# Gated mix of two attentions on one core: the first ten projection tiles take turns among four PSUM banks, the gate goes by the Pool engine and a transfer, and the main part's banks get pools of their own

## The chip, the cores and the metric

The kernel runs on one core of a Trainium2 chip. The time is the device time of that core in microseconds; lower is better. The engines are the tensor engine (PE, with its weight loads PEld), the vector engine (DVE), the scalar engine (ACT), GpSimd (POOL) and the sync engine (SP), which issues nearly all DMA transfers. Each engine takes its own instructions in the order in which the program wrote them, and waits on semaphores for what others make.

## What is computed

One input x of 2048 positions by 448 features goes through two attention blocks of 16 heads of 28, and a gate mixes the two. Everything is float32.

```python
g = sigmoid((x * gate_w).sum(-1))              # one number per position
# A: local and dilated: each position sees 8 keys, 2 apart, backwards
a = softmax(q·k[pos - 2w], w = 0..7) v  @ wo_A
# B: full attention over all 2048 keys
b = softmax(q k^T / sqrt(28)) v  @ wo_B
out = g * a + (1 - g) * b
```

The matmuls run in a reduced format of float32, so a product is made from a high and a low part of each operand: high times high, high times low, low times high.

## The kernel before

The order of every engine's work is written out by hand (`manual_schedule`); the program text is the order. There are three stages.

**Stage 1, projections.** 92 tiles are made one after another. Tiles 0 to 27 are queries and keys of B (128 rows by 512 positions each), 28 to 43 the values of B, 44 to 91 queries, keys and values of A (128 positions by 448 columns). The first ten (`FULL = 10`) are projected whole by `project`: eleven products of 128 rows, in the order of the lists `FIRST` (tile 0) or `ORDER`. Product (a, c, k) multiplies part a of x (0 high, 1 low) with part c of the weights, piece k of the 448 features; piece 3 is the tail of 64 features, whose high and low parts lie in the two halves of one tile. From tile 10 on, `project_halves` makes two chains of products of 64 rows that run beside each other, and mixes in matmuls of a first pass over the scores (`s1_half`, line 141), whose row maxima DVE takes (line 158). That first pass needs the keys, which have gone to DRAM and come back as `KH` (`load_k`).

A tile's result lies in a PSUM tile of two banks. There are four of them, `PS[0]` to `PS[3]`, named r0 to r3 in the profile's instructions (the page leaves the number out). Projections use r0 and r1 in turn (`PJ`), the first pass r2 and r3 (`PM`). A result of the first ten tiles leaves by `qk_tile`: ACT copies the high part (line 332), DVE makes the low part (line 333), SP stores both. Later results leave by one ACT copy (lines 337 and 351) and POOL adds the two halves (lines 339 and 352).

Before a tile can run, its operands must be split: `split` copies the high part on ACT (line 206) and subtracts on DVE or POOL (line 207). `split_x(nb)` does this for a quarter of x, its tail last (lines 232, 234); `split_third` for the third group of columns of the first weights. In program order `split_third` stands ahead of tile 1, `split_x(1)` ahead of tile 0's products. 13 matmuls on zeros (line 197) run while the first operands are still on their way.

**The gate.** The sums of the sigmoid come out of tiles 44 to 59 into `zt`. After tile 64, ACT makes exp(-z) and exp(z) (line 493), DVE adds 1 and inverts, twice (lines 494, 495); this gives `g_t` and `omg` = 1 - g, 128 by 16. After tile 68, PE transposes `omg` into the bank pair of the next tile, ACT copies it out (line 500), SP stores it to DRAM (`og_scr`, line 501) and loads it back in another layout, `og`, by 16 transfers (line 504). `load_q(0)` for the main part follows after tile 69.

**Stage 2, the main part.** 16 units of 16 steps make B's attention: score matmuls (line 1000), the exponential on ACT (line 1003), the sums over the values (`do_av`, line 962), with the rest of the first pass beside them, and A's attention on POOL and DVE. Its PSUM tiles T (three pairs of banks and a single one) come from one pool that takes the place of r0 to r3; `av` has the eighth bank. `RP[0]` is the pair that lies on r2, `RP[1]` that on r0, `TP` that on r1; T1 and av lie on r3.

**Stage 3** makes the output projection.

## Time and profile before

| what | value |
|---|---|
| time, median of 3 runs | 930.05 us (928.61 to 930.82) |
| the profiled execution's own time | 928.69 us |
| its span, first to last instruction | 926.9 us |
| busy share PE, DVE, ACT, POOL | 99%, 79%, 70%, 67% |
| mean granted clock of PE | 0.997 |
| stage 1 | 0 to 259 us |

In the views below, a row gives the start in us, the time it took in us, the engine, the line, the operation, what it writes and reads with shapes, how many instructions were merged (x4), and in square brackets the idle time of the engine before it and what ended that. "r" is a PSUM tile of stage 1, "T" one of the main part. In a row of windows stand the window, its length, and the busy time with the number of instructions for PE, then the granted share of PE's clock, the share of the DMA engines and GB/s.

### The profile page before, as it was taken

What the parts mean: (1) busy time and instruction counts of PE and PEld (TensorE: products, weight loads), DVE (VectorE), ACT (ScalarE), POOL (GpSimd) and SP (SyncE); (2) the same over time, 40 slices, a digit from 0 to 9 for tenths busy, and PEclk for the clock granted to TensorE, in tenths of its full rate; (3) what the DMA queues carried; (4) which work ended last, traced back from release to release, by engine and by line L of the source; (5) the groups of instructions that cost most, each with busy time, mean ns of one, the idle gap of its engine ahead of it and who ended that gap; (6) DMA issues with size and microseconds to landing.
All of it is one profiled execution on the core that took longest, in us unless ns stands there. A gap on an engine that the chain in (4) does not pass through costs nothing.

```text
span 926.9 us, 21402 instructions
## 1 busy us (share of the span) xinstructions
PE 914.1 (99%) x8398; PEld 545.6 (59%) x8398; DVE 733.3 (79%) x979; ACT 651.7 (70%) x802; POOL 620.8 (67%) x483
## 2 busy tenths in 40 slices
PE   8999999999999999999999999999999999999998
PEld 6899999989944444444444444444444444466667
DVE  5588999989969999999999999999998888500012
ACT  5456434333368888888888888888989889855551
POOL 2389846454469699999999999999994851300100
PEclk9999999999999999999999999999999999999999
DMA  9877402545362341336135232421312123553422
GB/s 285 263 232 196 156 12 81 152 100 147 85 239 62 95 125 45 85 104 134 41 92 152 88 101 60 133 82 30 106 42 53 33 62 99 149 159 110 135 88 91
DMA packets 101222, 104.36 MB, mean 113 GB/s; under 512 B 61732, under 2 KB 71348, under 8 KB 100336
## 3 DMA queue, kind: packets, MB, share of 16 engines
q1 hardware_dynamic: 100976, 102.72, 38.5%
q8 instruction: 66, 1.08, 0.5%
q10 hardware_dynamic: 144, 0.26, 0.1%
q14 instruction: 36, 0.29, 0.1%
HBM read 61.99 MB, written 40.48 MB: 111 GB/s over the span
## 4 chain that ended last, share of the span: by engine, by line
PE 92%; DMA 3%; ACT 2%; SPq 2%; DVE 1%; issue 1%; POOL 0%; ACTq 0%; DVEq 0%; POOLq 0%
PE T L1000 30%; PE av L962 26%; PE r L290 15%; PE T L801 8%; PE r L285 5%; PE r L141 4%; PE T L141 4%; DMA qk_hi<-qkh 1%; ACT P L1003 1%; SPq L98 1%; PE T L779 1%; DMA V<-in_xT 1%; DMA onlo<-on_lo 1%; DMA KH<-qk_hi 0%; DVE MX L145 0%
## 5 line engine op out<-in xcount | busy, mean ns | idle before, releaser
L1003 ACT ACTIVATE P<-T 128x1024 f32<-128x1024 f32 x512 | 497.1, 1024 | 91.9 <-PE T L1000 90.3
L145 DVE TENSOR_REDUCE MX<-T 128x1 f32<-128x512 f32 x470 | 443.4, 954 | 42.0 <-PE T L141 16.8
L962 PE MATMUL av<-P,V 128*32 128x512 f32 x2048 | 273.6, 606 | 0.0
L1000 PEld LDWEIGHTS T<-QH,KH 30*128 30x128 f32 x1024 | 91.0, 182 | 231.2 <-ACT P L1003 199.8
L1000 PE MATMUL T<-QH,KH 30*128 30x512 f32 x1024 | 220.9, 492 | 2.9 <-ACT P L1003 1.6
L141 PE MATMUL T<-KH,QP 28*128 28x512 f32 x704 | 222.0, 461 | 0.0
L158 DVE TENSOR_REDUCE MX<-r 128x2 f32<-128x1024 f32 x160 | 191.6, 1222 | 25.4 <-PE r L141 20.9
L1000 PE MATMUL T<-QH,KL 28*128 28x512 f32 x1024 | 188.7, 394 | 0.0
L1000 PE MATMUL T<-QL,KH 28*128 28x512 f32 x1024 | 187.3, 393 | 0.0
L597 POOL TENSOR_TENSOR prod<-qt,kt 128x896 f32<-128x896 f32 x64 | 135.2, 2116 | 5.6 <-DMA kt<-a_scr 5.2
L351 ACT ACTIVATE raw<-r 128x896 f32<-128x896 f32 (+1 forms) x64 | 58.9, 921 | 99.0 <-PE r L290 99.0
L652 POOL TENSOR_TENSOR oat<-oat,prod 128x896 f32<-128x896 f32 x56 | 118.1, 2109 | 2.4
L141 PEld LDWEIGHTS T<-KH,QP 28*128 28x128 f32 x704 | 86.2, 182 | 23.4 <-ACT P L1003 14.0
L352 POOL TENSOR_TENSOR ast<-raw 128x448 f32<-128x448 f32 x48 | 55.5, 1157 | 60.5 <-ACT raw L351 47.7
L647 POOL TENSOR_TENSOR prod<-vt,L 128x896 f32<-128x896 f32 x56 | 95.4, 1704 | 0.6
L141 PE MATMUL r<-KH,QP 64*128 64x512 f32 x320 | 94.2, 391 | 1.2 <-DVE MX L158 0.7
L1000 PEld LDWEIGHTS T<-QL,KH 28*128 28x128 f32 x1024 | 92.8, 185 | 0.0
L1000 PEld LDWEIGHTS T<-QH,KL 28*128 28x128 f32 x1024 | 92.0, 183 | 1.0
L290 PE MATMUL r<-wh,xh 64*128 64x448 f32 (+1 forms) x512 | 86.7, 363 | 1.0 <-ACT omT L500 1.0
L962 PEld LDWEIGHTS av<-P,V 128*32 128x32 f32 x2048 | 40.3, 108 | 78.8 <-issue 73.9
L789 DVE TENSOR_TENSOR oalo<-T,oah 128x384 fp32r<-128x384 f32 x16 | 8.9, 558 | 90.9 <-ACT onhi L788 82.3
L290 PE MATMUL r<-wh,xl 64*128 64x448 f32 (+1 forms) x384 | 70.8, 363 | 0.0
(111 smaller groups left out, 1148.3 us busy)
## 6 DMA issues: line engine op xcount, KB each, us to landing
a_scr<-ast SPq DMA_DIRECT2D x24, 448.0 KB
qk_hi<-qkh SPq DMA_DIRECT2D x24, 256.0 KB
qk_lo<-qkh SPq DMA_DIRECT2D x24, 256.0 KB
rbc<-rs SPq DMA_DIRECT2D x60, 64.0 KB
QP<-qk_hi SPq DMA_DIRECT2D x64, 56.0 KB
KL<-qk_lo SPq DMA_DIRECT2D x16, 224.0 KB
QH<-qk_hi SPq DMA_DIRECT2D x64, 56.0 KB
QL<-qk_lo SPq DMA_DIRECT2D x64, 56.0 KB
```

The source lines that it names most:

```text
L141: nc.tensor.matmul(bank, qhis[u][h % 2][r, 128 * qs:128 * qs + 128], KH[u // NB % 3][r, 512 * kc:512 * kc + 512], start=True, stop=True)
L145: nc.vector.tensor_reduce(MX[:, n % NMX:n % NMX + k], bank, axis=X, op=ALU.max)
L158: nc.vector.tensor_reduce(m, PM[k], axis=X, op=ALU.max)
L290: nc.tensor.matmul(bank[:, 0:cols], x, ws[c][rows, k, 0:cols], start=first, stop=last)
L351: nc.scalar.activation(raw[:, :, 0:cols], PJ[n % 2][:, :, 0:cols], AF.Copy)
L597: nc.gpsimd.tensor_tensor(out=p, in0=qt[c], in1=kvt["k", c % 2][:, HALO - DIL * w:HALO - DIL * w + NJ, :], op=ALU.mult)
L647: nc.gpsimd.tensor_tensor(out=dst.rearrange("p j (h d) -> p j h d", d=DH), in0=kvt["v", c % 2][:, HALO - DIL * w:HALO - DIL * w + NJ, :].r ...
L652: nc.gpsimd.tensor_tensor(out=oat[c], in0=oat[c], in1=oat[c, w], op=ALU.add)
L801: writes(bank, nc.tensor.matmul(bank[:, :D], src, wo[c][:, k, :], start=(first and k == ks[0] and i == 0), stop=(last and k == ks[-1] and ...
L962: nc.tensor.matmul(av[32 * h:32 * h + 32, :], V[:, kt, 4 * g + h, :], tiles_[h], start=(kt == 0), stop=(kt == NJ - 1), skip_group_check=True)
L1000: nc.tensor.matmul(bank[a], (KH[g % 3], KH[g % 3], KL[g % 2])[t][r, ks], (qh, ql, qh)[t][r, :], start=(t == 0), stop=(t == 2))
L1003: nc.scalar.activation(p, RP[0] if a == "2" else mine, AF.Exp, scale=SCALE)
```

## The change

1. **Four banks.** The first ten tiles use `PS[n % 4]` in place of `PJ[n % 2]`.
2. **Order at the start.** The 13 matmuls on zeros become 9, then the first product of tile 0, then 3. `FIRST` alternates high and low weights and puts the tail's products last. The third piece of the first x is cast by ACT, not DVE; DVE makes the three low parts first and the tail's after them. `split_third` stands ahead of tile 0's products, `split_x(1)` behind tile 0's result.
3. **First pass, first tile.** In tile 11 (`S1_START`) the score matmuls stand four (the first of each chain) and one (the second) products later.
4. **Gate.** POOL adds the 1 (it reads it from V, which holds ones there); one inversion stands after tile 66, one after tile 68; the transpose and ACT's copy go; `omg` is stored as it lies, element by element, after tile 70; the 16 loads of `og` stand after tile 73, `load_q(0)` after tile 76.
5. **Pools.** T[0], T[1], T[2] have a pool each; T1 and av share one.

```diff
-    def banks(shapes, ctx_):
-        pool = ctx_.enter_context(tc.tile_pool(name=f"t{len(T)}", bufs=1, space=bass.MemoryType.PSUM))
-        T[:] = [pool.tile([128, *x, 512], F32, name=f"T{len(x)}_{i}") for i, x in enumerate(shapes)]
+    def banks(n):
+        for i in range(n):
+            pool = ctx.enter_context(tc.tile_pool(name=f"t{i}", bufs=1, space=bass.MemoryType.PSUM))
+            T.append(pool.tile([128, 2, 512], F32, name=f"T{i}"))
...
-    for _ in range(13):
-        nc.tensor.matmul(PM[1][:, 1, :], t0[:, 128:256].bitcast(F32R), t0.bitcast(F32R), start=True, stop=True)
+    def warm(n):
+        for _ in range(n):
+            nc.tensor.matmul(PM[1][:, 1, :], t0[:, 128:256].bitcast(F32R), t0.bitcast(F32R), start=True, stop=True)
+
+    warm(9)
...
-        FIRST = [(a, c, k) for a, c in ((0, 0), (0, 1)) for k in range(3)] + [
-            (1, 0, 0), (0, 0, 3), (0, 1, 3), (1, 0, 1), (1, 0, 2)]
+        FIRST = [(0, 0, 0), (0, 1, 0), (0, 0, 1), (0, 1, 1), (0, 0, 2), (0, 1, 2),
+                 (1, 0, 0), (1, 0, 1), (1, 0, 2), (0, 0, 3), (0, 1, 3)]
...
-            bank = PJ[n % 2][:, half or 0, :]
+            bank = PS[n % 4][:, 0, :] if half is None else PJ[n % 2][:, half, :]
...
                 product(n, p, None, i == 0, i == len(order) - 1)
+                if n == 0 and i == 0:
+                    warm(3)
...
                         if s1[m - n]:
-                            l[8:8] = [(m, s1_half, (1, half))]
-                            l[2:2] = [(m, s1_half, (0, half))]
+                            late = m == S1_START
+                            l[8 + late:8 + late] = [(m, s1_half, (1, half))]
+                            l[2 + 4 * late:2 + 4 * late] = [(m, s1_half, (0, half))]
...
-                bank = PJ[n % 2][:, 0, :]
+                bank = PS[n % 4][:, 0, :]
...
-        for kt in range(3):
+        for kt in range(2):
             nc.vector.tensor_copy(xh[0][:, kt, :], r[:, kt, :])
+        nc.scalar.activation(xh[0][:, 2, :], r[:, 2, :], AF.Copy)
...
-            if n == 1:
+            if n == 0:
                 split_third()
-            if n in (0, 3, 5):
-                split_x((n + 1) // 2 if n else 1)
+            if n in (3, 5):
+                split_x((n + 1) // 2)
...
                 a_tile(n, t[2], t[3])
+            if n == 0:
+                split_x(1)
...
             if n == 64:
+                gate = []
                 for sgn, dst in ((-1.0, g_t), (1.0, omg)):
                     e = sp.tile([128, NJ], F32, name="ez")
                     nc.scalar.activation(e, zt, AF.Exp, scale=sgn)
-                    nc.vector.tensor_scalar(e, e, 1.0, None, op0=ALU.add)
-                    nc.vector.reciprocal(dst, e)
-            if n == 68:
-                b = PJ[(n + 1) % 2][:, 0, :]
-                nc.tensor.transpose(b[0:NJ, 0:128], omg, ident)
-                t = wp.tile([NJ, 128], F32, name="omT", bufs=1)
-                nc.scalar.activation(t, b[0:NJ, 0:128], AF.Copy)
-                nc.sync.dma_start(og_scr.rearrange("(j p) -> j p", j=NJ), t)
+                    nc.gpsimd.tensor_tensor(out=e, in0=e, in1=V[:, 0, :, DH], op=ALU.add)
+                    gate.append((dst, e))
+            if n in (66, 68):
+                nc.vector.reciprocal(*gate.pop(0))
+            if n == 70:
+                nc.sync.dma_start(og_scr.rearrange("(j p) -> p j", j=NJ), omg)
+            if n == 73:
                 for b in range(NB):
...
-            if n == 69:
+            if n == 76:
                 load_q(0)
...
-    banks([(2,), (2,), (2,), ()], ctx)
+    banks(3)
     RP = T[2], T[0]
-    TP, T1 = T[1], T[3]
-    av = ctx.enter_context(tc.tile_pool(name="psv", bufs=1, space=bass.MemoryType.PSUM)).tile(
-        [128, 512], F32, name="av")
+    TP = T[1]
+    pool = ctx.enter_context(tc.tile_pool(name="psv", bufs=1, space=bass.MemoryType.PSUM))
+    T1 = pool.tile([128, 512], F32, name="T1")
+    av = pool.tile([128, 512], F32, name="av")
```

PE at the start, before: the zeros (r3 from t0), then tile 0 into r0, tile 1 into r1, tile 2 into r0 again. xh0 and xl0 are the high and low part of the first quarter of x, wh0 and wl0 those of the weights.

```order
L197 MATMUL r3_140<-t0_161 128x512 x13
L285 MATMUL r0_128<-xh0_184,wh0_192 128x512 x3
L285 MATMUL r0_128<-xh0_184,wl0_193 128x512 x3
L285 MATMUL r0_128<-xl0_188,wh0_192 128x512
L285 MATMUL r0_128<-xh0_184,wh0_192 128x512
L285 MATMUL r0_128<-xh0_184,wl0_193 128x512
L285 MATMUL r0_128<-xl0_188,wh0_192 128x512 x2
L285 MATMUL r1_132<-xh0_184,wh0_192 128x512 x4
L285 MATMUL r1_132<-xh0_184,wl0_193 128x512 x4
L285 MATMUL r1_132<-xl0_188,wh0_192 128x512 x3
L285 MATMUL r0_128<-xh0_184,wh0_192 128x512 x4
```

The same place now:

```order
L200 MATMUL r3_140<-t0_161 128x512 x9
L290 MATMUL r0_128<-xh0_180,wh0_188 128x512
L200 MATMUL r3_140<-t0_161 128x512 x3
L290 MATMUL r0_128<-xh0_180,wl0_189 128x512
...
L290 MATMUL r0_128<-xl0_184,wh0_188 128x512 x3
L290 MATMUL r0_128<-xh0_180,wh0_188 128x512
L290 MATMUL r0_128<-xh0_180,wl0_189 128x512
L290 MATMUL r1_132<-xh0_180,wh0_188 128x512 x4
...
L290 MATMUL r2_136<-xh0_180,wh0_188 128x512 x4
...
L290 MATMUL r3_140<-xh1_181,wh0_188 128x512 x4
```

Tile 0's tail products now end its list, and tile 2 begins in r2, which no result holds, where before it began in r0.

ACT at the same place, before: the weights' first group (raw), the second quarter of x (xh1), tile 0's result (qkh from r0), then the third weights.

```order
L206 ACTIVATE wh0_192<-raw_196 128x128 x3
L206 ACTIVATE xh1_185<-V_146 128x512 x3
L232 ACTIVATE xh1_185<-V_146 128x512
L332 ACTIVATE qkh_257<-r0_128 128x512
L206 ACTIVATE wh0_192<-raw_196 128x128 x3
L206 ACTIVATE wh0_192<-wt0_195 128x128
L332 ACTIVATE qkh_281<-r1_132 128x512
```

And now:

```order
L211 ACTIVATE wh0_188<-raw_192 128x128 x6
L211 ACTIVATE wh0_188<-wt0_191 128x128
L340 ACTIVATE qkh_256<-r0_128 128x512
L211 ACTIVATE xh1_181<-V_146 128x512 x3
L237 ACTIVATE xh1_181<-V_146 128x512
L340 ACTIVATE qkh_280<-r1_132 128x512
```

The third weights moved ahead of tile 0's result, the second quarter of x behind it.

PE at the change from stage 1 to the main part, before, with the semaphores that are waited for (DMAHW are transfers): the last projection, then the first step.

```order
L290 MATMUL r_132<-wh_2344,xl_191 128x448 x6
L1000 MATMUL T_2_3284<-QH,KH_151 128x512 [waits DMAHW3_49,DMAHW4_49,DVE_49,Activation_49]
L1000 MATMUL T_2_3284<-QH,KH_151 128x512 [waits DMAHW5_49]
L141 MATMUL T_3_3285<-KH_152,QP_157 128x512 [waits DMAHW0_49]
L1000 MATMUL T_0_3282<-QH,KH_151 128x512 [waits DMAHW6_49]
L141 MATMUL T_1_3283<-KH_152,QP_158 128x512 [waits DMAHW1_49]
```

And now:

```order
L295 MATMUL r_132<-wh_2343,xl_187 128x448 x6
L1010 MATMUL T_3286<-QH,KH_151 128x512 [waits DMAHW4_49,DMAHW3_49,DVE_49]
L1010 MATMUL T_3286<-QH,KH_151 128x512 [waits DMAHW5_49]
L142 MATMUL T_3290<-KH_152,QP_157 128x512 [waits DMAHW6_49,DVE_49]
L1010 MATMUL T_3278<-QH,KH_151 128x512 [waits DMAHW6_49,Activation_49]
L142 MATMUL T_3282<-KH_152,QP_158 128x512 [waits Activation_49]
```

The first matmul no longer waits for ACT; the wait for ACT stands at the matmuls that write the pairs on r0 (T_3278) and r1 (T_3282).

## The prediction

> **What bounds the kernel now.** I read the page first (busy shares, then the chain), then PE's waits, then the timeline at the four places that the change touches, and last the windows of PE's clock.

> ```profile
> span 926.9 us, 21402 instructions
> PE 914.1 (99%) x8398; PEld 545.6 (59%) x8398; DVE 733.3 (79%) x979; ACT 651.7 (70%) x802; POOL 620.8 (67%) x483
> PE 92%; DMA 3%; ACT 2%; SPq 2%; DVE 1%; issue 1%; POOL 0%; ACTq 0%; DVEq 0%; POOLq 0%
> ```

> PE is busy for 914.1 of 926.9 us and carries 92% of the chain; 12.8 us are idle. The change removes no products, so it can only win idle time and time at a low clock. PE's waits (engine, tile, line, releaser: total us, count, longest) name what it aims at:

> ```profile
> PE T L1000 <- ACT P L1003: 1.6, 3, 1.0
> PE r L285 <- DVE qkh L333: 1.4, 1, 1.4
> PE T L1000 <- ACT raw L351: 1.0, 1, 1.0
> PE r L290 <- ACT omT L500: 1.0, 1, 1.0
> PE r L141 <- DVE MX L158: 0.7, 1, 0.7
> PE r L141 <- DMA KH<-qk_hi: 0.5, 1, 0.5
> ```

> **The start.** The timeline here shows the zeros, tiles 2 to 4, what is made for them, and the keys' way back:

> ```profile
> 1.46 5.62 PE L197 MATMUL r<-t 128*128 128x512 f32 x13 [1.46 <-DVE omg L195]
> ...
> 13.08 0.58 ACT L332 ACTIVATE qkh<-r 128x512 fp32r<-128x512 f32 x1
> 13.56 0.69 ACT L206 ACTIVATE wh<-raw 128x128 fp32r<-128x128 f32 x3
> 13.58 0.69 DVE L234 TENSOR_TENSOR xh<-V,xh 64x512 fp32r<-64x512 f32 x1
> 15.13 1.17 PE L285 MATMUL r<-xh,wh 128*128 128x512 f32 x4 [1.36 <-DVE qkh L333]
> 17.77 1.09 PE L285 MATMUL r<-xh,wh 128*128 128x512 f32 x4
> 20.31 1.09 PE L285 MATMUL r<-xh,wh 128*128 128x512 f32 x4
> ...
> 25.60 2.65 SPq L98 DMA_DIRECT2D QP<-qk_hi  x4
> ...
> 33.91 1.61 SPq L98 DMA_DIRECT2D KH<-qk_hi  x4
> 35.64 1.20 PE L285 MATMUL r<-xh,wh 64*128 64x512 f32 x8
> ...
> 39.69 0.47 PE L141 MATMUL r<-KH,QP 64*128 64x512 f32 x1 [0.55 <-DMA KH<-qk_hi]
> ```

> Tiles 2, 3 and 4 start at 15.13, 17.77 and 20.31; undisturbed one takes 20.31 − 17.77 = 2.54 us, 0.23 a product. Tile 2 waits 1.36 us for tile 0's low part in r0. With four banks that wait is gone. The earlier first product (a zero costs 5.62/13 = 0.43 us, and one real product now stands ahead of the last three) brings tile 1 forward by some 0.6 us. Against this, the third weights now stand ahead of tile 0's result on ACT, and the second quarter of x behind it, so tile 3, which needs the tail of that quarter (the 13.58 row's work), comes to wait. Its tail must follow ACT's weights (0.69) and tile 0's copy (0.58), and four casts: I put a new wait of about 1.2 us there, an estimate from these rows, and a gain of about 0.8 us at tile 4.

> That gain is not kept. At 39.69 PE waits for the keys, which go out to DRAM and back by SP's queue (25.60 to 33.91 and on). That row of loads and stores is paced by its own transfers and not by PE: PE has no wait between 20.31 and 39.14, and the order of SP's instructions there is as before. So I hold the keys' return at 39.69. What the start then gives is only what the moved score matmuls give: four pairs of 64-row products more run ahead of the wait, 4 × 0.23 = **0.9 us**. If PE comes there no earlier, only the 0.55 idle can be won; eight half products in the 35.64 row take 1.20, the other end, which the start's 0.8 + 0.55 would allow. Bounds 0.55 to 1.2.

> **The gate.** ACT's evacuations around it, DVE's two operations, and PE's waits above:

> ```profile
> 185.73 0.92 ACT L351 ACTIVATE raw<-r 128x896 f32<-128x896 f32 x1 [1.23 <-PE r L290]
> 201.29 0.92 ACT L351 ACTIVATE raw<-r 128x896 f32<-128x896 f32 x1 [2.96 <-PE r L290]
> ...
> 240.57 0.92 ACT L351 ACTIVATE raw<-r 128x896 f32<-128x896 f32 x1 [1.76 <-PE r L290]
> 256.24 0.92 ACT L351 ACTIVATE raw<-r 128x896 f32<-128x896 f32 x1 [1.70 <-PE r L290]
> ```

> From 240.57 to 256.24 there are six tiles, 2.61 us each. From 185.73 to 201.29 there are five and 15.56 us: 15.56 − 5 × 2.61 = 2.5 us more than undisturbed. The waits on MX (0.7) and omT (1.0) are 1.65 of it; the rest is the transpose itself and the refilling of PE after it.

> ```profile
> 187.00 0.25 DVE L495 RECIPROCAL g_t<-ez 128x16 f32<-128x16 f32 x1
> 187.16 0.85 DVE L494 TENSOR_SCALAR ez<-ez 128x16 f32<-128x16 f32 x1
> L177 POOL TENSOR_TENSOR nmt<-nmv,nmt 128x16 fp32r<-128x16 f32 x4 | 0.9, 224 | 0.0
> ```

> The 0.85 us step of DVE, which waited for ACT's exponential while row maxima stood behind it, goes to POOL. There it is two additions of 128x16, nearest the L177 row: 2 × 0.22 us on an engine on which the chain spends 0%. DVE keeps two inversions of 0.25 us, now two tiles apart and with their input long made. I cost them at nothing to 0.25 each on PE, hidden by the 0.92 us evacuation and the second pair of first-pass banks; without that cover they cost 0.5. The transpose and ACT's copy go entirely. Gain **2.3 us**, bounds 1.65 (idle rows alone, a refilled pipe counted at nothing) and 2.5.

> The price of the new store lies on SP's queue. It writes 2048 single elements, and no row shows such a store. Nearest are these:

> ```profile
> raw<-in_gw SPq DMA_DIRECT2D x3, 1.0 KB
> 91.29 2.77 SPq L258 DMA_DIRECT2D raw<-in_gw  x3
> ...
> 201.58 7.28 SPq L504 DMA_DIRECT2D og<-og_scr  x16
> ...
> 212.34 1.11 SPq L98 DMA_DIRECT2D QH<-nm  x2
> ```

> The gate's weights come in as 256 single numbers each (1.0 KB), 2.77/3 = 0.92 us of SP; eight times that is 7.4 us. A load of a query row (212.34, two in 1.11) takes 0.56, the other end. I take the upper end, as it is the row of the same kind. [...]

> What covers it: before, SP did nothing for the a_scr stores from 201.58 until 213.45 (16 loads, then load_q), 11.9 us, and PE has no wait after 198.39 till 259. Now 7.4 us stand behind tile 70, 7.3 behind tile 73, load_q behind tile 76, with 3 × 2.61 = 7.8 us between; no piece is longer than the 11.9 us that cost nothing before. So I cost it at 0, and `og` and QH are still in some 35 us before the main part.

> **The change of stage, and the clock.**

> ```profile
> 259.26 0.50 PE L1000 MATMUL T<-QH,KH 30*128 30x512 f32 x2 [1.01 <-ACT raw L351]
> 261.49 0.50 PE L1000 MATMUL T<-QH,KH 30*128 30x512 f32 x2 [1.02 <-ACT P L1003]
> ...
> 267.52 0.50 PE L1000 MATMUL T<-QH,KH 30*128 30x512 f32 x2
> ...
> 272.22 0.49 PE L1000 MATMUL T<-QH,KH 30*128 30x512 f32 x2
> 268.24 2.11 POOL L597 TENSOR_TENSOR prod<-qt,kt 128x896 f32<-128x896 f32 x1 [5.20 <-DMA kt<-a_scr]
> ```

> The first score matmul goes to the pair on r2, free for long, yet waited 1.01 us for the last evacuation (0.92 like the others), as all of T was one pool. With pools apart it starts at once, and the one pair that the evacuation holds (r1) is written only after the first step's other matmuls, 261.49 − 1.02 − 259.26 = 1.2 us of PE, longer than 0.92. Gain **1.0 us**, bounds 0.7 (some of it back as a wait there) to 1.2. The next wait, 1.02 us for the exponential, is no part of the change and stays.

> The two waits together have a consequence, which PE's clock shows (window: length, PE busy and count, granted clock, DMA share, GB/s):

> ```profile
> 261.00:262.00 1.00, 0.51 (x7) 1.00 0.63 185
> ...
> 262.50:263.00 0.50, 0.50 (x7) 0.60 0.88 193
> ...
> 265.50:266.00 0.50, 0.50 (x12) 0.50 1.05 395
> 266.00:266.50 0.50, 0.50 (x11) 0.98 0.99 374
> ```

> From 262.6 to 266.0 PE runs at half clock. The steps from 261.49 to 267.52 took 6.03 us; the next two (267.52 to 272.22) took 4.70: 1.3 us lost. It followed 2.03 us of waits within 3.3 us; the lone waits of 0.96 and 1.36 us earlier did not bring the clock down. With one of the two gone, I take the drop as gone: **1.3 us**, bounds 0 and 1.7 (half of 3.4).

> **Sum.** 0.9 + 2.3 + 1.0 + 1.3 = 5.5 us off this execution's 928.69 us (span 926.9 and 1.8 around it), 923.2. The median of the runs is 930.05, 1.36 above this execution: 930.05 − 5.5 = **924.5 us**. All of it lies in stage 1 or at its end; the main part's orders are alike, and PE waits there for nothing that I can see moved, so I carry it to the end.

> **Rivals.**

> *B, the clock still drops.* What speaks for it: one wait of 1.02 us stays at the same step, and before, PE was busy for only 0.51 of the time from 261 to 262. [...] Against it: the lone wait of 0.96 us had no drop. Without the 1.3 us: 925.8.

> *C, the gate's gain is given back.* The inversions still stand among the row maxima, and a wait on POOL or on MX (0.7 before) replaces the old one; or the first tiles' gain vanishes in the keys' return. One of the two largest terms gone: 924.5 + 2.3 = 926.8.

> *D, the end doesn't move.* POOL starts A's attention only at 268.24, after 5.20 us for kt from DRAM. If that row of transfers and POOL's 2.11 us operations paced the main part, what stage 1 wins would be idle there. Against it: POOL is 0% of the chain. Then only a few tenths stay: 929.5.

> *E, slower.* The store of single elements holds SP so long that the a_scr stores behind it keep their buffers, POOL and ACT stop, and PE with them. SP was held for 11.9 us at no cost; to lose the 5.5 us gained and the 1.9 of a measurable loss, it has to be held 19.3 us. That is 2.6 times my worst price for the store alone; or, if the store ran into the 16 loads, 12 us instead of 7.4. At twice 7.4 and the 7.3 of the loads it is 22 us, a stall of 10: 934.5. The SP row of in_gw speaks against it, unless single elements write slower than they read.

> **How the numbers follow.** A 0.42 (with its own range 923.3 to 925.3), B 0.25, C 0.13, D 0.10, E 0.05, and 0.05 that the start or the gate gives a microsecond more (923.0 and below). The likeliest is A, 924.5. The range runs from 922.3 (all upper ends: 1.2 + 2.5 + 1.2 + 1.7 = 6.6 off, and 1.1 for a start kept in part) to 928.2, which takes in A, B and C. 0.2% is 1.9 us, about what a measurement of this kernel can tell from no change: faster below 928.2 (A, B, C and the 0.05, less 0.01 for their spread) 0.84, the same (D) 0.10, slower (E and a little beside) 0.06.

> **What the profile after would show.** For the start: no wait of PE on qkh, a new one of about 1.2 us on the tail of xh near 16 to 17.6, and the wait on KH still there near 39.7, 0.5 to 1.0 us. If it stands earlier, I was wrong that the keys' transfers set it. For the gate: no omT, no wait on MX near 189, evacuations 2.6 apart throughout, and the row of the og_scr store. For the change of stage: no wait on raw above 0.2, the wait on P of 1.0 still there, the first score near 255, and PE's clock at 1.00 for the 15 us behind it. A second drop at that place would be B; a PE wait on POOL's or ACT's buffers between tiles 70 and 80, E.

## The result and the profile after

The changed kernel takes 930.14 us (median of 12 runs, 928.06 to 931.32) against 929.94 us before (12 runs beside it, 928.04 to 932.06). The ratio is 1.0003, with a 95% interval of 0.9993 to 1.0014: no change that can be measured. The profiled execution took 929.85 us.

In the views of the changed kernel L359 is ACT's evacuation of a tile (L351 before), L509 the store of omg, L513 the loads of og, L373 the a_scr stores, L1010 the score matmuls and L1013 the exponential. First its page: span, PE's share, and the chain by engine and by line.

```profile
span 927.6 us, 21400 instructions
PE 914.1 (99%) x8396; PEld 542.0 (58%) x8396; DVE 732.3 (79%) x976; ACT 651.9 (70%) x802; POOL 620.4 (67%) x485
PE 90%; DMA 5%; SPq 2%; ACT 2%; issue 1%; DVE 0%; POOL 0%; ACTq 0%; DVEq 0%; POOLq 0%
PE T L1010 29%; PE av L972 26%; PE r L295 12%; PE T L811 8%; PE r L290 6%; PE T L142 4%; PE r L142 4%; DMA og_scr<-omg 2%; ACT P L1013 1%; SPq L513 1%; PE T L789 1%; DMA raw<-in_wB 1%; DMA V<-in_xT 1%; DMA onhi<-on_hi 1%; DMA KH<-qk_hi 0%
```

PE is as busy as before, but 2% of the chain is now the transfer of omg, which was not in it, and 1% SP at the loads of og. PE's waits:

```profile
PE r L295 <- ACT raw L359: 2.4, 1, 2.4
...
PE T L1010 <- ACT P L1013: 1.3, 4, 0.6
PE r L290 <- DVE xh L239: 0.8, 1, 0.8
PE r L142 <- DMA KH<-qk_hi: 0.7, 1, 0.7
```

The waits on qkh, MX, omT and, at the change of stage, raw are gone as forecast; that on the exponential is now 1.3 us in four pieces. A new one of 2.4 us on an evacuation stands in the middle of stage 1. SP's timeline, the chain (start, us, what), and SP's wait show where it comes from:

```profile
204.14 0.53 SPq L509 DMA_DIRECT2D og_scr<-omg  x1
206.36 0.36 SPq L373 DMA_DIRECT2D a_scr<-ast  x1
218.25 8.39 SPq L513 DMA_DIRECT2D og<-og_scr  x16
```

```profile
204.14 14.09 DMA og_scr<-omg
```

```profile
SPq L513 <- DMA og_scr<-omg: 11.5, 1, 11.5
```

The store costs SP only 0.53 us, but the data take 14.09 us to land, and the first load of og waits for them: 11.5 us in which SP issues nothing, then 8.4 us of loads. The a_scr stores stand behind, so their buffers don't come free, and ACT can't evacuate at 230.44 and 240.83. (The wait that ends at 217.34 is another one, for PE; e2 shows it.)

```profile
212.02 0.92 ACT L359 ACTIVATE raw<-r 128x896 f32<-128x896 f32 x1 [1.61 <-PE r L295]
217.34 0.92 ACT L359 ACTIVATE raw<-r 128x896 f32<-128x896 f32 x1 [3.91 <-remote]
...
230.44 1.73 ACT L359 ACTIVATE raw<-r 128x896 f32<-128x896 f32 x2 [5.61 <-DMA a_scr<-ast]
...
240.83 0.92 ACT L359 ACTIVATE raw<-r 128x896 f32<-128x896 f32 x1 [2.91 <-DMA a_scr<-ast]
```

What the DMA engines do meanwhile is in the windows (window, length, granted clock, DMA share, GB/s): they are full, and move 17 GB/s.

```profile
204.00:206.00 2.00, 1.00 0.69 189
...
208.00:212.00 4.00, 1.00 1.40 17
212.00:216.00 4.00, 1.00 1.33 18
```

The packets of SP's queue (number, MB, share of the 16 engines) tell with what they are full: first from 206 to 208, then from 208 to 216, last from 208 to 212 in e1, which stores rows in place of single elements.

```profile
q1 hardware_dynamic: 2469, 0.18, 119.9%
```

```profile
q1 hardware_dynamic: 306, 0.14, 136.6%
```

```profile
q1 hardware_dynamic: 1131, 0.36, 38.6%
```

The single elements are among the 2469 packets of the first two us. In the eight us behind them only 306 packets move. They are 448 bytes each, so they belong to the a_scr store issued at 206.36, and each holds an engine for 0.57 us (1.366 × 16 × 8 / 306); in e1 a packet takes 0.02 us (0.386 × 16 × 4 / 1131). So the elements' own packets pass quickly, and what stands behind them hardly moves until they have landed. Why isn't shown.

An account of both kernels and of the experiments follows from ACT's rows, one evacuation for each of the 92 tiles and the exponentials behind them. The table gives by how many us each stretch came out longer (+) or shorter than in the profile before. The kernels e1 to e11 are described below.

| stretch | after | e1 rows | e2 late og | e5 pools | e6 start | e9 DVE | e11 gate |
|---|---|---|---|---|---|---|---|
| to tile 11 (start) | +0.04 | +0.38 | +2.22 | +0.81 | −0.44 | +0.31 | +0.40 |
| tile 65 to 74 (gate) | −2.47 | −2.47 | −2.47 | +0.05 | +0.07 | −2.45 | −2.47 |
| tile 74 to 91 (store) | +4.18 | +0.11 | +0.78 | −0.01 | −0.01 | −0.05 | +6.40 |
| tile 91 to the first exponential (pools) | −1.17 | −1.17 | −1.17 | −1.17 | 0.00 | −1.15 | 0.00 |
| first to fifth exponential (clock) | +0.39 | +0.38 | −1.16 | −1.13 | −0.13 | −1.17 | −1.53 |

So the gate and the pools gave what they should, the store took more than that back, the start came out even, and the clock fell just the same. The store's stretch differs between executions: e3 and e4, which have the same store, show +3.56 and +5.10 (e4's with a half clock in it).

### The profile page after: what moved, and what is told of

It reads as the page before. It is cut to its first block, busy times and chain, and to the rows that moved or that the text cites. A ratio compares the mean times of both kernels' runs of the same rounds, so it can differ in the third digit from the quotient of the medians.

```text
span 927.6 us, 21400 instructions
## 1 busy us (share of the span) xinstructions
PE 914.1 (99%) x8396; PEld 542.0 (58%) x8396; DVE 732.3 (79%) x976; ACT 651.9 (70%) x802; POOL 620.4 (67%) x485
## 4 chain that ended last, share of the span: by engine, by line
PE 90%; DMA 5%; SPq 2%; ACT 2%; issue 1%; DVE 0%; POOL 0%; ACTq 0%; DVEq 0%; POOLq 0%
PE T L1010 29%; PE av L972 26%; PE r L295 12%; PE T L811 8%; PE r L290 6%; PE T L142 4%; PE r L142 4%; DMA og_scr<-omg 2%; ACT P L1013 1%; SPq L513 1%; PE T L789 1%; DMA raw<-in_wB 1%; DMA V<-in_xT 1%; DMA onhi<-on_hi 1%; DMA KH<-qk_hi 0%
## 5 line engine op out<-in xcount | busy, mean ns | idle before, releaser
L1013 ACT ACTIVATE P<-T 128x1024 f32<-128x1024 f32 x512 | 496.9, 1024 | 90.9 <-PE T L1010 90.0
L1010 PEld LDWEIGHTS T<-QH,KH 30*128 30x128 f32 x1024 | 91.0, 182 | 229.8 <-ACT P L1013 199.2
L1010 PE MATMUL T<-QH,KH 30*128 30x512 f32 x1024 | 221.2, 492 | 1.5 <-ACT P L1013 1.3
L1010 PE MATMUL T<-QH,KL 28*128 28x512 f32 x1024 | 188.9, 393 | 0.0
L1010 PE MATMUL T<-QL,KH 28*128 28x512 f32 x1024 | 187.9, 393 | 0.0
L359 ACT ACTIVATE raw<-r 128x896 f32<-128x896 f32 (+1 forms) x64 | 58.8, 920 | 101.0 <-PE r L295 88.5
L142 PEld LDWEIGHTS T<-KH,QP 28*128 28x128 f32 x704 | 86.2, 182 | 23.3 <-ACT P L1013 12.8
L1010 PEld LDWEIGHTS T<-QL,KH 28*128 28x128 f32 x1024 | 92.8, 185 | 0.0
L1010 PEld LDWEIGHTS T<-QH,KL 28*128 28x128 f32 x1024 | 92.1, 183 | 1.0
L142 PE MATMUL r<-KH,QP 64*128 64x512 f32 x320 | 85.6, 391 | 1.4 <-DMA KH<-qk_hi 0.7
L295 PE MATMUL r<-wh,xh 64*128 64x448 f32 (+1 forms) x512 | 84.2, 363 | 2.4 <-ACT raw L359 2.4
```

Source lines behind the costliest of these rows:

```text
L142: nc.tensor.matmul(bank, qhis[u][h % 2][r, 128 * qs:128 * qs + 128], KH[u // NB % 3][r, 512 * kc:512 * kc + 512], start=True, stop=True)
L295: nc.tensor.matmul(bank[:, 0:cols], x, ws[c][rows, k, 0:cols], start=first, stop=last)
L359: nc.scalar.activation(raw[:, :, 0:cols], PJ[n % 2][:, :, 0:cols], AF.Copy)
L1010: nc.tensor.matmul(bank[a], (KH[g % 3], KH[g % 3], KL[g % 2])[t][r, ks], (qh, ql, qh)[t][r, :], start=(t == 0), stop=(t == 2))
L1013: nc.scalar.activation(p, RP[0] if a == "2" else mine, AF.Exp, scale=SCALE)
```

## Experiments

The times of the kernel before beside them are 929.90 (e1 to e4, 23 runs), 929.69 (e5 to e8, 29 runs) and 929.63 us (e9 to e11, 17 runs). Ratios have their 95% interval.

**e1, the store as rows.**

```diff
-                nc.sync.dma_start(og_scr.rearrange("(j p) -> p j", j=NJ), omg)
+                nc.sync.dma_start(og_scr.rearrange("(p j) -> p j", j=NJ), omg)
```

> The changed kernel, with the store of omg as 128 rows of 16 elements that lie together, where the change writes 2048 single elements (og_scr then holds the gate in another order, so B's share is weighted by other positions' gates; the work is the same). Theory: the single elements take 14 us to land, SP waits 11.5 us for them at the first og load, and that costs PE 4.1 us between tile 74 and tile 91. Then with rows that wait is about 3 us, tiles 70 to 91 stay 2.3 to 2.5 us ahead of the kernel before, and the span falls from 927.6 to about 923.5. Rival: the wait is one for the place in SP's row (16 loads of 8.4 us, then load_q, now in the middle of the a_scr stores), whatever the store is: then 2 us or more of the 4.1 stay and the span is above 925.5.

924.20 us, 0.9943 (0.9927 to 0.9958). SP's store and its wait at og:

```profile
204.47 0.53 SPq L509 DMA_DIRECT2D og_scr<-omg  x1
```

```profile
SPq L513 <- DMA og_scr<-omg: 0.6, 1, 0.6
```

The same 8 KB at the same place in SP's row, in 128 pieces in place of 2048: the wait falls from 11.5 to 0.6 us, and the stretch from tile 74 to 91 from +4.18 to +0.11. So the single elements cost it, not the place of the loads.

**e2, the loads of og later.**

```diff
-            if n == 73:
+            if n == 79:
                 for b in range(NB):
```

> The changed kernel, with the 16 loads of og behind tile 79 in place of 73; the store of single elements stays behind tile 70. Theory of the head of the line: what hurts is that SP stands 11.5 us at the first og load with the a_scr stores behind it; with the loads 15 us later the store has landed, SP waits for nothing, and the 4.1 us come back (span about 923.5). Theory of the shared queues: the a_scr stores that are issued behind 2048 single elements land late whatever SP does, so ACT and POOL run out of buffers just the same, and 2 us or more stay (span above 925.5, PE's wait on raw of about 2.4 us still there near 215).

925.35 us, 0.9950 (0.9935 to 0.9966). With single elements still, but nothing on SP that waits for them, the stretch costs +0.78 in place of +4.18. So 3.4 us went with the head of SP's line. What is left is no want of buffers. It arises by tile 77, where ACT waits for PE:

```profile
218.27 0.92 ACT L359 ACTIVATE raw<-r 128x896 f32<-128x896 f32 x1 [2.68 <-PE r L142]
```

This is the wait that the changed kernel has till 217.34. Measured against e1's evacuations, tile 77 is 0.6 to 1.5 us late in every kernel with the single store of 2048 elements (after, e2, e3, e4, e11), and not late in any without it. No wait that the traces name explains why PE is late there. The pages count instruction queues among the DMA queues (q8 with 65 packets and q14 with 36 in the changed kernel), and a packet of q8 that e1 has at 211.8 us came at 218.6 in the changed kernel; whether it was for PE, and whether it held PE, is not shown. The span expected (923.5) was missed by these 0.8 us and by a start that was 2.2 us late in this execution; this profile had no half clock.

**e3, the splits at the start at their old places.** `split_third` ahead of tile 1 and `split_x(1)` ahead of tile 0's products, as before; all else as changed.

> The changed kernel, with the third weights and the second quarter of x split at their old places in the program (third weights ahead of tile 1, second quarter ahead of tile 0's products). Theory of the order: the changed order holds ACT from tile 0's copy until the third weights have come (14.38 in place of 13.08), its stores and all of SP's row behind them come about 1 us later, and so the keys: undone, the keys' wait ends near 39.7 again or earlier and tile 11 is evacuated 0.9 us or more before 42.51; the span falls by about 1. Theory of the transfers: the loads at the start only landed up to 1 us later in that one execution; then this run shows tile 11 no earlier than runs e1 and e2, which have the changed order.

928.37 us, 0.9986 (0.9973 to 1.0000). Tile 11 came 0.31 earlier than before, and ahead of the four profiles with the changed order known then (+0.04 to +2.22). The ratio, too, lies below the changed kernel's (1.0003, 0.9993 to 1.0014), though the intervals overlap. By this alone the order costs something; e10 did not bear it out.

**e4, four filling matmuls ahead of the second step.**

```diff
+            if st == 1:
+                for _ in range(4):
+                    nc.tensor.matmul(av, KH[0][:, 0:128], KH[0][:, 0:512], start=True, stop=True)
```

> The changed kernel, with four matmuls of 512 columns more on PE ahead of the second step of the main part, into the bank of the sums that nothing uses yet (their result is overwritten). They fill the 0.56 us in which PE waits for the exponential there; 4 x 0.23 = 0.92 us. Theory of the gaps: the half clock from 263.9 to 267.3 is the answer to this idle time, and with it filled the clock stays at 1.00: the steps behind it take 2.35 us each and 1.3 us are won, less 0.4 for what of the filler does not fit the gap, so about 926.7 and a mean clock of 0.999. Rival: the drop belongs to the change of stage itself (matmuls of 28 to 30 rows in place of 64) and comes with no gap too: then the span is 927.6 to 928.1 and the half clock is there again.

928.56 us, 0.9984 (0.9974 to 0.9995). The profile had no half clock at the change of stage, but one 30 us earlier, behind the stall of the store (windows of PE: window, length, busy and count, clock, DMA share, GB/s):

```profile
228.00:230.00 2.00, 0.77 (x7) 1.00 0.94 273
230.00:232.00 2.00, 0.99 (x8) 0.92 0.91 227
232.00:234.00 2.00, 2.00 (x12) 0.50 0.78 188
...
262.00:264.00 2.00, 1.90 (x14) 1.00 0.79 229
264.00:266.00 2.00, 2.00 (x26) 1.00 0.86 227
```

So in this execution the store's stall cost a second time, by the clock. The expected mean of 0.999 in this run was missed for that reason (0.998).

**e5, the pools alone,** on the kernel before.

> The kernel before, with the main part's banks in pools of their own and nothing else. The prediction's step: the first score matmul no longer waits 1.01 us for the last evacuation, and with one of the two waits gone the half clock is gone as well: every run at a mean clock of 0.999 or more, median about 929.9 - 1.0 - 1.0 = 927.9 (the kernel before has the drop in 14 of 23 runs, so its median holds it). Rival, now the likelier: the drop needs only the wait for the exponential that stays; the gain is 1.0 to 1.1 us, the runs still divide into clocks of 1.0 and 0.998 about 1.8 us apart, median about 928.9.

928.27 us, 0.9984 (0.9975 to 0.9993). The first exponential comes 1.17 us earlier, measured from tile 91. Of 12 runs 6 had a mean clock of 0.999 or more (926.74 to 928.15 us) and 6 one of 0.997 or 0.998 (928.4 to 930.1). The rival stands: with one of the two waits gone a drop still comes in half of the runs, where the kernel before has one in 41 of 69. The mean clock doesn't tell where in the run it came; the one profile of e5 has none.

**e6, the start alone,** on the kernel before.

> The kernel before, with the changes of the start alone (four banks, order of zeros, products and splits, late score matmuls of tile 11). The prediction's step: tile 11 is evacuated 0.9 us earlier than 42.51, median 929.0. Theory from the four profiles with the changed start (42.55, 42.90, 44.73, 42.81): the third weights hold ACT, the stores and the keys come later by as much as the late matmuls win, tile 11 at 42.5 to 43.5, and the median is 929.9 or up to 0.8 above it. Everything from tile 64 on (gate, pools, half clock) is as in the kernel before.

928.04 us, 0.9984 (0.9975 to 0.9993): 1.5 us faster (0.7 to 2.3), which my theory from four profiles did not have; the prediction's 0.9 lies inside the interval. Tile 11 came 0.44 us earlier in its profile, not 0.9. The keys' wait and the first chain piece behind the loads:

```profile
PE r L141 <- DMA KH<-qk_hi: 0.8, 1, 0.8
```

```profile
7.23 5.57 DMA raw<-in_wB
```

In the profile of the changed kernel the same piece of the chain reads as follows, 0.7 us longer.

```profile
7.29 6.25 DMA raw<-in_wB
```

**e7, the store in four parts** behind tiles 70, 72, 74 and 76, og behind tile 80, with the splits of e3 and the filler of e4.

```diff
+            if n in (70, 72, 74, 76):
+                q = slice(2 * n - 140, 2 * n - 136)
+                nc.sync.dma_start(og_scr.rearrange("(j p) -> p j", j=NJ)[:, q], omg[:, q])
+            if n == 80:
```

> The changed kernel with four edits: the store of omg in four parts of 512 elements behind tiles 70, 72, 74 and 76, the loads of og behind tile 80, the splits at the start at their old places (as in e3), and the four filling matmuls (as in e4). If the losses are what the first runs showed (4.1 us of the store, of which e2 left 0.7; 0.3 or more of the start; the half clock 1.8 us in the runs that have it), the gate's 2.4 us stay through tile 91, no PE wait on raw is left, every run has a clock of 0.999 or more, and the median is about 928.4 (the kernel before at clock 1.0) - 2.4 - 1.1 - 0.3 + 0.3 for the filler = 924.9 or below, down to 923.5. Rival: parts of the store stand in the queues behind each a_scr store and each costs some of what the whole did: above 926.

934.70 us, 1.0053 (1.0036 to 1.0070): slower, and not by the little that I gave the rival. From tile 74 to 91 it lost 9.4 us (tile 74 came 1.89 us earlier than in the kernel before, tile 91 7.47 us later). SP's waits and the DMA windows:

```profile
SPq L99 <- DMA a_scr<-ast: 7.9, 2, 6.5
SPq L373 <- DMA a_scr<-ast: 5.3, 1, 5.3
SPq L508 <- DMA og_scr<-omg: 1.7, 1, 1.7
```

```profile
212.00:216.00 4.00, 1.00 1.16 12
216.00:220.00 4.00, 1.00 1.80 127
220.00:224.00 4.00, 1.00 1.03 5
```

With a part behind every a_scr store, it is the a_scr stores that land late, and SP waits for them 13 us. Why parts of 512 elements hold the engines so long was not settled.

**e8, the filler alone,** on the kernel before.

> The kernel before, with the four filling matmuls ahead of the second step and nothing else. The wait of 1.01 us for the last evacuation stays, that of 1.02 for the exponential is filled with 0.92 us of work. Theory of the share of idle time: PE's idle time within some 3.4 us falls from 2.0 to 1.0 us, and the drop is gone in all runs: clock 1.0 throughout, median about 928.4 (that of the runs before at clock 1.0). Rival, a single wait of 1 us at this place is enough: the runs divide as before, median near 929.9.

928.68 us, 0.9988 (0.9976 to 0.9999). 7 of 12 runs at 0.999 or more, against 28 of 69. The profile had no drop at the change of stage, although PE was busy there for 2.99 of 4 us only (260 to 264), but one at the start, behind tile 2's wait, which was 2.3 us in this execution (1.4 in the one before):

```profile
16.26 2.03 PE L285 MATMUL r<-xh,wh 128*128 128x512 f32 x4 [2.31 <-DVE qkh L333]
```

```profile
12.87:16.28 3.41, 1.10 (x6) 1.00 1.08 304
16.28:19.70 3.42, 3.42 (x8) 0.50 1.03 311
```

The two chains tell why it was longer; the first is of the kernel before, the second of e8, with the same code at this place. The load of the second quarter of x took 1.1 us more, and what follows came later by that; the half clock came on top:

```profile
5.20 5.76 DMA V<-in_xT
```

```profile
5.19 6.89 DMA V<-in_xT
```

**e9, the store by a transpose on DVE, with the filler.**

```diff
-                nc.sync.dma_start(og_scr.rearrange("(j p) -> p j", j=NJ), omg)
+                t = sp.tile([128, 32], F32, name="omt", bufs=1)
+                nc.vector.transpose(t, omw)
+                for c in range(4):
+                    nc.sync.dma_start(og_scr.rearrange("(j c p) -> c j p", j=NJ, c=4)[c], t[32 * c:32 * c + NJ])
```

Here omg is the left half of a tile omw of 32 columns.

> The changed kernel with two edits: DVE transposes omg in blocks of 32 x 32, so that it is stored as 4 transfers of 16 rows of 128 bytes in the right order; and the four filling matmuls of e4. Theory: the store lands in about 3 us as in e1, tiles 66 to 91 keep the gate's 2.4 us, and with the stall near 215 gone and the wait at the second step filled there is no half clock in stage 1 or at its end: at least 11 of 12 runs at a mean clock of 0.999 or more, and a median of 924.2 (e1, which had the drop in 2 of 6 runs) - 0.6 = 923.6. Rival on the clock: the drop comes by chance with the waits that stay; then some 4 of 12 runs are at 0.998 and the median is 924.2 or above.

924.20 us (923.55 to 924.86), 0.9941 (0.9923 to 0.9959): faster than both kernels, with og_scr in the order in which og is read. A DVE transpose of 128x32 takes 0.20 us (L182 of the kernel before, the same shape). The four stores take SP 2.31 us, the waits for them 1.1 us, and PE goes through the end of stage 1 without idle time or drop:

```profile
204.62 2.31 SPq L513 DMA_DIRECT2D og_scr<-omt  x4
```

```profile
260.00:262.00 2.00, 2.00 (x27) 1.00 1.01 308
262.00:264.00 2.00, 2.00 (x25) 1.00 1.02 333
```

All 6 runs are at 0.999 or 1.0. The time is 0.6 above what was expected, less than e1's own runs are apart (922.79 to 926.12), so what the filler adds to e1 is not told by these times, only by the clock.

**e10, e9 with the splits at their old places.**

> e9, with the splits at the start at their old places (as in e3), on the same chip. If the changed order of the splits costs what the profiles hint (tile 11 at 42.21 with the old order, 42.07 to 44.73 with the new one), this is 0.3 to 0.7 faster than e9; if it is the transfers' landing alone that moves tile 11, the two are the same within 0.5 us.

925.12 us, 0.9950 (0.9930 to 0.9969). No faster than e9; 3 of 6 runs have a clock of 0.998, and the profile's drop lies at 16 to 20 us, behind a wait of PE on the third weights of 2.0 us. So what e3 hinted at is not borne out here; with the store of single elements it stays open.

**e11, the gate alone,** on the kernel before, with the store of single elements.

> The kernel before with the changes of the gate alone (POOL adds, the inversions apart, no transpose, the store of single elements, later loads of og and load_q). From the profile after: tiles 69 to 74 come 2.4 us earlier, and then 4.1 us are lost at the store, so tile 91 is about 1.7 us late; with the second stall, half clock near 231 in part of the runs. Median 929.7 + 1.7 + up to 1 = 931.4 to 932.4. Rival: the store's 4.1 us belong to the four banks and the shift of the start; then it is near 928.

931.74 us, 1.0019 (1.0007 to 1.0032): slower alone, as expected.

```profile
PE r L290 <- ACT raw L351: 2.6, 1, 2.6
```

```profile
SPq L504 <- DMA og_scr<-omg: 10.5, 1, 10.5
```

The stall is the same without the four banks and the pools, and 11 of 12 runs have a clock of 0.998 or less. In its profile the drop came at 230 us, lasted 6.8 us, and none came at the change of stage, so the store's stretch shows +6.40.

## Why the prediction was wrong

*The start, −0.9.* About right in size, but not by its reasoning. The step that held the keys' return at 39.69 failed: it came at 40.66, the late matmuls won their 0.9, and tile 11 stayed at +0.04. The new wait on the tail was 0.8 us (1.2 forecast). But the keys move with the loads at the start, by up to 2 us from one execution to the next with the same code. With the start as before, tile 11 came at 0, +0.81, +3.37 and +0.40 (before, e5, e8, e11), 1.1 on the mean; with the changed one at +0.04, +0.38, +2.22, +0.30, −0.44 and +0.31 (after, e1, e2, e4, e6, e9), 0.5. The one profile that I argued from was the earliest of the four. Alone the change of the start is worth 1.5 us (0.7 to 2.3, e6), and which of its parts gives this was not taken apart; four banks also take away the wait of up to 2.3 us behind which the clock fell in e8.

*The gate, −2.3.* Right: −2.45 to −2.47 in every kernel that has it.

*The store, 0.* This is the step that failed. I priced the time that SP is busy with the issue (7.4 us from the in_gw row) and looked for what covers that. The issue took 0.53. What counts is the landing, 14.09 us, since the loads of og wait for it. SP's waits of the kernel before have the row that shows this kind of wait, for the store of 16 rows, and I did not use it:

```profile
SPq L504 <- DMA og_scr<-omT: 2.8, 1, 2.8
```

The cover of 11.9 us was then exceeded: 11.5 of waiting and 8.4 of loads are 19.9 us in one piece. It cost 4.18 us by the account (e1: +0.11 with rows): against e1, 1.4 by tile 77, where PE itself was late, and 2.6 at tile 79, where the buffers did not come free. In the profiles of e4 and e11 it brought a half clock as well. By the element the landing is 6.9 ns (14.09 us / 2048), where I had put 3.6 ns of SP's time (7.4 us / 2048).

*The change of stage, −1.0.* Right: −1.15 to −1.17 in all kernels with the pools.

*The clock, −1.3.* Wrong; rival B was right. The drop at the change of stage came again. The first fence is of the kernel before, the second of the changed one; each has the 3.41 us ahead of the drop and the drop:

```profile
259.19:262.60 3.41, 2.32 (x30) 1.00 0.83 242
262.60:266.02 3.42, 3.42 (x24) 0.50 1.01 298
```

```profile
260.43:263.84 3.41, 2.65 (x34) 1.00 0.68 198
263.84:267.26 3.42, 3.42 (x25) 0.50 0.98 246
```

I took the drop for a fixed answer to 2 us of waits. Two things were wrong in that. In these profiles the clock changes in steps of 3.41 us (shown under the last heading), and the step ahead of the drop began at 259.19, when the first of the two waits (258.25 to 259.26) was all but over: of the 1.09 us in that step without work, 1.02 are the wait that stays. The changed kernel, which does not have the first wait, has the drop too, behind a step with 0.76 us without work: the wait that stays was enough. And it does not come in each execution: 41 of 69 runs of the kernel before have a mean clock below 0.999, at 929.3 us and up, and 28 have not, at 927.0 to 929.5; of the changed one 11 of 12 have, and the one run at 1.0 took 928.06. With PE never idle at the change of stage (e9) all 6 runs kept the clock.

*Rival E* named the mechanism: the store did run into the loads and hold SP. Its threshold was even passed (19.9 us, where it asked for 19.3), but E let every us beyond 11.9 reach PE, which makes 8.0, and 4.2 did; so the gains were eaten and the kernel was not slower. *Rival D* has the time that is nearest (929.5), and that is luck: in e9 the first exponential came 3.2 us earlier than before and the span was 4.2 us shorter, so what stage 1 wins does reach the end. Of *rival C* the half on the gate did not come about: its gain was there at tile 74, and no wait on MX took its place. The other half, the start's gain lost in the keys' return, is what this one profile shows (+0.04), but not e6's runs.

*The sum:* the store's 4.2 and the clock's 1.3 are the 5.5 us that were forecast. e5, e6 and e11, the three parts alone, give −1.4, −1.7 and +2.1 by their medians, −1.0 together; the whole measured +0.2, with an interval of −0.7 to +1.3. With the store mended (e9) the kernel is at 924.2, where the forecast of 924.5 had put it. That agreement is partly luck: e1, without the filler that wins what the clock was to give, is at 924.2 too.

## What to carry to other kernels

The store had two prices here, the queue's time to issue it (0.53 us) and the time until it had landed (14.09); the second is the one to put in the sum where a later instruction of the queue waits for it, as the first load of og did for 11.5 us with the a_scr stores held behind it. A wait or a clock that one profile shows may be one draw of several: look at the clock and the span of every run before counting a stall as won, and take the start of a kernel from more than one execution (here tile 11 came at 0 to +3.37 us with the same code, and the load of the second quarter of x took 5.76 us in one profile, 6.89 in another). Where a layout has to be turned for a small store, try a transpose in 32 x 32 blocks on an engine with time to spare in place of single elements (e9, on DVE: −0.05 in place of +4.18 us).

## What was not expected of the hardware

2048 stores of 4 bytes took 14.09 us to land, though their own packets had passed within two (206 to 208), and the 448 KB behind them moved at 17 to 18 GB/s from 208 to 216. Cutting them into four made it worse (+9.4 us against +4.18).

```profile
11.69:15.10 3.41, 2.31 (x11) 1.00 1.11 318
15.10:18.51 3.41, 2.45 (x11) 1.00 1.05 254
```

In stage 1 the profiles divide cleanly by PE's busy time in a step. Six steps with 1.10 to 1.66 us of work were followed by half clock (e4, e7 twice, e8, e10, e11), and none with 1.71 us or more (after, 229.71 to 233.12). At the change of stage this does not hold: there steps with 1.8 to 2.7 us of work were followed by it (before, after, e1, e3, e6), and two steps of 2.4 us in e11 were not. Whether that has to do with the matmuls there, of 28 to 30 rows in place of 64, was not tested.
